# Attention and two MLPs on one core: p stays unnormalised and becomes the stationary operand of P V

## The chip, the cores and the metric

The kernel runs on one core of a Trainium2 chip. The time is the device time of one execution in microseconds (us), and the median of several runs counts. The core has five engines that work side by side: TensorE (PE) for matrix products, VectorE (DVE), ScalarE (ACT), GpSimd (POOL), and SyncE (SP), which here only starts transfers. Each engine takes its own instructions in the order in which they stand in its queue. PE writes its products to PSUM, eight banks of 128 partitions by 512 f32 columns; DVE and ACT read them there. A matrix product loads one operand into PE first (the stationary one, a weight load), and then streams the columns of the other (the moving one) past it.

## The reference

There are 4 batches, 8 heads, 576 positions and 64 columns to a head. Causal attention with a decay goes into two MLPs of 2304 tokens, one after the other:

```python
decay = cum[:, :, :, None] - cum[:, :, None, :]        # cum = cumsum(log(clip(f)))
scores = np.where(causal, -1e9, scale * q @ k.T + decay)
attn = np.exp(scores - scores.max(-1))
attn = attn / (attn.sum(-1) + 1e-09)
x = (attn @ v)                                         # to 2304 x 512
h = x @ w_in                                           # 512 -> 2048
x = (np.maximum(h, 0) + alpha * np.minimum(h, 0)) @ w_out
out = ((x @ w_a) * (x @ w_b)) @ w_o                    # 512 -> 1536 -> 512
```

## The kernel before

The program has three parts: attention together with the first 7 of the 16 column blocks of the first MLP (up to about 362 us; the MLP of the last batch follows until about 412), the other 9 blocks, and the second MLP. The change touches attention alone.

The 32 heads run through slots `u`, one head to a slot. A head has five blocks of queries: 0 to 3 with 128 queries each, and a rest of 64 that is worked on together with the rest of the head's pair (block 4, two heads, 128 rows). For a block, PE makes the scores (`sc`, `scr`), DVE masks them and finds the greatest (line 375, it writes `s` and `nm`), and ACT takes exp of `s` and sums the rows into `sm` (line 376). In the next slot `rinv` makes the reciprocal of the sums, `p_hi` scales `s` by it, and `p_lo` brings P into the form that P V needs: keys on partitions. There are two ways.

- The first ten heads (`NATIVE`) work in f32: `p_hi` scales `s` in place on POOL or ACT, `p_lo` calls `p_whole`, where PE transposes P block by block (`tp`) and ACT or DVE copies it out of PSUM into `PT`. `pv_whole` holds V as the stationary operand (64 columns of V and 64 zeros, so that the two heads of a pair fall on the two halves of the partitions of one bank) and streams P's columns.
- The other 22 heads split P into two f16 parts: `p_hi` writes `s * ri` (times 2^15) as f16 (line 428 on ACT for blocks 2 and 3, line 430 on POOL for 0, 1 and 4), `p_lo` writes what is left of it (line 510, DVE), and a transfer transposes both (line 517). V is split into three bf16 parts by POOL (line 329). `pv` holds two parts of V as the stationary operand and streams P's columns, three matmuls to a block; the result has V's columns on partitions, in two half sums that ACT (line 565) and DVE (line 566) add. For a pair of heads ACT copies the sum to `xh` (line 236), and POOL writes what rounding left to `xl` (line 572).

P V runs two slots behind its head (`LAG`). x then lies with its 512 columns on partitions, and the MLP takes it so: three matmuls in f32r to a product (`mm3`, lines 666 to 668), `leaky` for the sloped step (lines 660 to 663), and `ys` (line 708) out of PSUM.

What runs in which order is set in three layers. Four lists in `_P` (`even0` and `odd0` for the first ten slots, `even` and `odd` for the rest) name the steps of a slot: `s0` to `s3` scores and exp of a block, `R` those of the rest, `ri` and `rr` the reciprocals, `h0` to `h4` and `l0` to `l4` the two halves of P, `p0` and `p1` P V, `T`, `Q`, `V`, `vs` loads and splits, `W` one of 14 weights of the MLP (a transfer, a step of ACT at line 129, three of DVE, then ACT and POOL), `M` the place where MLP steps go in from slot 10 on. `rates` says how much of the MLP goes into a slot. The compiler's scheduler then sets the order of each engine's queue by these places and by its own estimate of when things are ready.

Of the kernel before, what the change touches and what calls it, by code (L numbers as in the profile page):

```python
# [8 lines left out]
F32 = mybir.dt.float32  # L9
# [17 lines left out]
ST = 512  # L27
# [10 lines left out]
    even="ri T h3 h2 h0 s2 vs M h1 Q s0 M l2 s3 M s1 l1 M l0 l3 p0 p1 V po M W".split(),  # L38
    odd="ri h3 h2 h0 R rr vs h1 M Q l2 T l3 s2 M h4 s3 l1 M M s1 l0 s0 p0 p1 V W po l4 M".split(),
# [44 lines left out]
def decay_attention_then_two_mlps(ctx, tc, q, k, v, f, w_in, w_out, alpha, w_a, w_b, w_o, out):  # L84
# [157 lines left out]
    def attention_setup():  # L242
# [19 lines left out]
        for i in range(2):  # L262
# [53 lines left out]
    def load_v(n):  # L316
        b, h = divmod(n, H)
        vs = ap_["vs", n % 3]
        i = 3 if n < NATIVE and n % 2 == 0 else 1
        sp.dma_start(vs[:, 0:4, i], v[b, h, 0:ST].rearrange("(t p) d -> p t d", p=128))  # L320
        sp.dma_start(vs[0:SR, 4, i], v[b, h, ST:])

    def split_v(n):

        if n < NATIVE:
            return
        vs = ap_["vs", n % 3]
        for i in range(1, 3):
            eng(f"v{i}", "pool").tensor_tensor(vs[:, :, i + 1], vs[:, :, i], high(vs[:, :, i]), op=ALU.subtract)
# [20 lines left out]
    def s_view(n, i):  # L350
        if i == 4:
            return ap_["sr"]
        o = {3: 0, 2: 512, 1: 896, 0: 1152}[i]
        return ap_["s", n % 2][:, o:o + 128 * (i + 1)]
# [109 lines left out]

    def pv_whole(u, c):

        g, j = divmod(u, 2)
        vs = ap_["vs", u % 3]
        vz = vs[:, :, 0:2] if j else vs[:, :, 3:5]
        vz = vz.rearrange("p t i d -> p t (i d)")  # L470
        if j == 0:
            ps_x[g, c] = ps["mm"].tile([128, 512], F32, tag="mm", name=f"pvw_{g}_{c}")
        ps_o = ps_x[g, c]
        pt = P32[u, ("lo", "hi")[c]]
        w = 256 + SR * c
        todo_ = []
        for t in range(2 * c + 1):
            b0 = 2 * t + c
            todo_.append((ps_o[:, 0:256].rearrange("p (i n) -> p i n", i=2), t, pt[:, b0:b0 + 2]))
        t = 2 * c + 1  # L480
        todo_.append((ps_o[:, 128:256], t, pt[:, 0 if c else 2]))
        if c == 1:
            qs = slice(SR * j, SR * j + SR)
            for t in range(NQ):
                todo_.append((ps_o[:, 256:w], t, P32[u | 1, "r"][:, t, qs]))
        for m, (o, t, p) in enumerate(todo_):
            first, last = j == 0 and m == 0, j == 1 and m == len(todo_) - 1
            pe.matmul(o, vz[:, t], p, start=first, stop=last, skip_group_check=True)
        if j == 0:
            return  # L490
        b, hp = divmod(g, NP)
        x_tiles(b)
        xh, xl = (x_[:, hp, 256 * c:256 * c + w] for x_ in X[b])
        act.activation(xh, ps_o[:, :w], AF.Copy, scale=1.0 / PSCALE)
        dve.scalar_tensor_tensor(xl, ps_o[:, :w], 1.0 / PSCALE, f32(xh), op0=ALU.mult, op1=ALU.subtract)
# [9 lines left out]
    def p_lo(n, i):  # L505
        if n < NATIVE:
            return p_whole(n, i)
        t, s, ri = p16.pop((n, i))
        g, o = GROUP[i]
        eng(f"l{i}", "dve").scalar_tensor_tensor(t[:, 1::2, :], s, ri, t[:, 0::2, :], op0=ALU.mult, op1=ALU.subtract)  # L510
        whole, done_ = p16[n, g]
        done_.append(i)
        if g == "r" or len(done_) == 2:
            PT[n, g] = ap_["a2"].tile(
                [128, GSIZE[g], 128], F16, tag=f"PT_{g}", name=f"PT_{n}_{g}", bufs=2 if g == "r" else LAG,
            )
            sp.dma_start_transpose(out=PT[n, g], in_=whole.rearrange("p t n -> p (t n)"))
            del p16[n, g]
# [570 lines left out]
```

## Time and profile before

| | us |
|---|---|
| median of 3 runs | 1061.34 (1060.59 to 1064.08) |
| the profiled execution | 1064.5 |
| its span in the profile | 1062.7 |
| PE busy | 1006.4 (95%) |
| weight loads busy | 942.2 (89%) |
| DVE busy | 715.6 (67%) |
| ACT busy | 474.2 (45%) |
| POOL busy | 465.9 (44%) |

Busy times are of the profiled execution, shares are of its span. A busy share is a mean over stages, and a wait that an engine ended is put down to the one that came last. Records of PE overlap: the length of one holds the time until its last result is out, so what one costs in a row of them is the step from one start to the next. An f32 product stands as two records.

### The profile page before, as it was taken

How to read it: one execution, taken by the hardware profiler on the slowest of the kernel's cores; microseconds unless marked ns; L12 is line 12 of the kernel's file. 1: busy time of each engine (PE TensorE's matmuls, PEld its weight loads, DVE VectorE, ACT ScalarE, POOL GpSimd, SP SyncE). 2: the span in 40 equal slices, each digit the busy share in tenths (PEclk: the TensorE clock that was granted, in tenths of full speed). 3: DMA queues.
4: the chain of work that ended last, by engine and by line, in shares of the span. 5: the costliest groups of instructions: out<-in, count | busy, mean ns of one | idle time of the engine just before them, and what ended most of it. 6: DMA issues, size and time to landing. Idle time of an engine off the chain costs nothing.

```text
span 1062.7 us, 17909 instructions
## 1 busy us (share of the span) xinstructions
PE 1006.4 (95%) x6255; PEld 942.2 (89%) x6255; DVE 715.6 (67%) x1463; ACT 474.2 (45%) x1090; POOL 465.9 (44%) x503
## 2 busy tenths in 40 slices
PE   4899899998998999999999998999999999999998
PEld 2777789988898898999999998899989999899997
DVE  5667899679878466444456659755985658965553
ACT  4666788577776554333343443322432113321110
POOL 5344556355455355333456767522543224531111
PEclk9999999999999999999999999999999999999999
DMA  6654588888797676756667996726238383353623
GB/s 137 162 140 152 141 166 169 210 169 170 191 170 155 192 241 209 236 191 191 197 223 263 346 360 237 317 90 239 96 100 317 113 309 121 120 204 142 248 89 109
DMA packets 193582, 202.71 MB, mean 191 GB/s; under 512 B 103956, under 2 KB 160788, under 8 KB 193492
## 3 DMA queue, kind: packets, MB, share of 16 engines
q1 hardware_dynamic: 193492, 201.57, 63.2%
q8 instruction: 49, 0.80, 0.3%
q14 instruction: 41, 0.34, 0.1%
HBM read 133.32 MB, written 50.17 MB: 173 GB/s over the span
## 4 chain that ended last, share of the span: by engine, by line
PE 54%; DVE 7%; DMA 4%; issue 2%; ACT 2%; POOL 2%; SPq 0%; DVEq 0%; ACTq 0%; POOLq 0%
PE p L666 7%; PE p L668 7%; PE p L667 7%; PE o L668 4%; PE o L666 4%; PE o L667 4%; PE ya L666 3%; PE ya L667 3%; PE ya L668 3%; PE hb L668 3%; PE hb L667 3%; PE hb L666 3%; DMA wr_in<-in_moe_w_in 1%; DMA wr_out<-in_moe_w_out 1%; POOL yhl L873 1%
## 5 line engine op out<-in xcount | busy, mean ns | idle before, releaser
L666 PE MATMUL p<-yq,w_h 128*128 128x384 f32 x360 | 121.9, 339 | 2.2 <-DVE lu L1035 1.3
L668 PE MATMUL p<-yq,w_h 128*128 128x384 f32 x360 | 121.3, 337 | 0.0
L667 PE MATMUL p<-yq,w_h 128*128 128x384 f32 x360 | 121.2, 337 | 0.0
L1017 POOL TENSOR_TENSOR gg<-tc,gg 128x384 fp32r<-128x384 f32 x36 | 36.6, 1017 | 113.5 <-ACT gg L1016 96.4
L666 PE MATMUL o<-w_o,gg 128*128 128x512 f32 x216 | 84.7, 393 | 1.7 <-ACT gg L1016 1.7
L376 ACT ACTIVATE s<-s,nm 128x256 f32<-128x256 f32 (+3 forms) x128 | 71.0, 556 | 31.0 <-DVE nm L375 30.5
L667 PE MATMUL o<-w_o,gg 128*128 128x512 f32 x216 | 84.8, 393 | 0.0
L668 PE MATMUL o<-w_o,gg 128*128 128x512 f32 x216 | 83.2, 393 | 0.0
L663 POOL TENSOR_TENSOR gb<-lt,gb 128x384 fp32r<-128x384 f32 x54 | 55.7, 1032 | 60.0 <-ACT gb L662 59.9
L1017 POOL TENSOR_TENSOR gg<-td,gg 128x384 fp32r<-128x384 f32 x36 | 38.0, 1056 | 89.9 <-ACT gg L1016 84.2
L1016 ACT CAST gg<-tc 128x384 fp32r<-128x384 f32 x36 | 18.5, 514 | 124.3 <-DVE tc L1015 123.8
L666 PEld LDWEIGHTS p<-yq,w_h 128*128 128x128 f32 x360 | 67.6, 188 | 7.1 <-DVE lu L1035 1.7
L666 PE MATMUL ya<-gb,w_out 128*128 128x384 f32 x216 | 71.2, 337 | 2.8 <-ACT gb L662 1.6
L667 PE MATMUL ya<-gb,w_out 128*128 128x384 f32 x216 | 72.7, 337 | 0.0
L668 PE MATMUL ya<-gb,w_out 128*128 128x384 f32 x216 | 72.5, 336 | 0.0
L666 PE MATMUL h<-xh,w_in 128*128 128x288 f32 x224 | 66.9, 303 | 5.8 <-ACT ys L708 2.6
L667 PEld LDWEIGHTS p<-yq,w_h 128*128 128x128 f32 x360 | 67.6, 188 | 3.7
L661 DVE SCALAR_TENSOR_TENSOR lt<-lu,nal,hb 128x384 f32<-128x384 f32 x54 | 33.0, 611 | 55.9 <-ACT lu L660 54.2
L663 POOL TENSOR_TENSOR g<-lt,g 128x288 fp32r<-128x288 f32 x56 | 51.0, 916 | 39.0 <-ACT g L662 37.8
L668 PEld LDWEIGHTS p<-yq,w_h 128*128 128x128 f32 x360 | 67.6, 188 | 0.2
L667 PE MATMUL y<-g,w_out 128*128 128x288 f32 x224 | 65.8, 299 | 1.1 <-POOL g L663 1.1
L667 PE MATMUL h<-xl,w_in 128*128 128x288 f32 x224 | 66.1, 296 | 0.0
(202 smaller groups left out, 3238.7 us busy)
## 6 DMA issues: line engine op xcount, KB each, us to landing
yq<-yq_d SPq DMA_DIRECT2D x49, 768.0 KB
yq_d<-yhl SPq DMA_DIRECT2D x42, 384.0 KB
yl<-ya_d SPq DMA_DIRECT2D x48, 192.0 KB
po_d<-os SPq DMA_DIRECT2D x36, 256.0 KB
os<-po_d SPq DMA_DIRECT2D x36, 256.0 KB
wr_in<-in_moe_w_in SPq DMA_DIRECT2D x16, 512.0 KB
wr_out<-in_moe_w_out SPq DMA_DIRECT2D x16, 512.0 KB
RK<-in_k SPq DMA_DIRECT2D x44, 144.0 KB
```

The source lines that it names most:

```text
L376: act.activation(s, s, AF.Exp, bias=nm, scale=-1.0, accum_out=sm)
L661: dve.scalar_tensor_tensor(t, u, nal[:, fi:fi + 1], hp[:, :n], op0=ALU.mult, op1=ALU.add)
L663: pool.tensor_tensor(gl, t, f32(gh), op=ALU.subtract)
L666: pe.matmul(o, lh, rh, start=start, stop=False)
L667: pe.matmul(o, lh, rl, start=False, stop=False)
L668: pe.matmul(o, ll, rh, start=False, stop=stop)
L873: pool.tensor_tensor(yh[:, 1], x, f32(yh[:, 0]), op=ALU.subtract)
L1016: ap_["last"] = act.copy(g[:, 0], o).ins
L1017: pool.tensor_tensor(g[:, 1], o, f32(g[:, 0]), op=ALU.subtract)
```

## The change

P stays as exp left it, and the division comes behind P V. P is now the stationary operand: `pv` loads a block of transposed P (128 keys by 128 queries) and streams 64 columns of V, so x comes out with queries on partitions. All blocks of a head fall into one bank. DVE scales them out of PSUM by the reciprocal, which now has a value to each partition (`xn`), and the rest's 64 rows of each head into one quarter of `xr`. A new step `X`, a slot after a pair's last P V, calls `turn`: PE transposes `xn` (four blocks of 128x128) and multiplies `xr` with `fold`, which puts the two heads' halves side by side; ACT and DVE write `xh` and `xl` out of PSUM. In heads 0 to 9 `p_hi` does nothing. In the others it is one step for blocks 2 and 3 (`hi`, 896 columns, ACT), one for 0 and 1 (`lo`, 384, ACT) and one for the rest (`r`, POOL), and `p_lo` has the same three on DVE. V loses its zeros. The lists in `_P` place the steps anew, and one more slot runs at the end.

```diff
-    even="ri T h3 h2 h0 s2 vs M h1 Q s0 M l2 s3 M s1 l1 M l0 l3 p0 p1 V po M W".split(),
+    even="T h3 h2 h0 h1 s2 vs M Q X s0 M l3 l2 s3 ri M s1 l1 l0 M p0 p1 V M W".split(),
-    eng={'xl': 'pool', 'h2': 'act', 'h3': 'act', 'h0': 'pool', 'h1': 'pool', 'x': 'dve'},
+    eng={'hi': 'act', 'lo': 'act', 'r': 'pool'},
...
+            ap_["xr", i] = a.tile([128, 128], F32, tag=f"xr_{i}", name=f"xr_{i}")
+            zeros(ap_["xr", i])
+        fold = ap_["fold"] = a.tile([128, 64], F32, name="fold")
+        pool.tensor_tensor(fold, ap_["ident"][:, 0:64], ap_["ident"][:, 64:128], op=ALU.add)
...
-            ap_["vs", i] = a.tile([128, NQ, 5, D], F32, tag=f"vs_{i}", name=f"vs_{i}")
-            zeros(ap_["vs", i][:, :, 0::4])
-            zeros(ap_["vs", i][SR:, 4, 1:4])
+            ap_["vs", i] = a.tile([128, 3, NQ, D], F32, tag=f"vs_{i}", name=f"vs_{i}")
+            zeros(ap_["vs", i][SR:, :, 4])
...
     def p_hi(n, i):
...
-                act.activation(s, s, AF.Copy, scale=ri)
...
+        p16.setdefault((n, g, "hi"), []).append(i)
+        if g != "r" and len(p16[n, g, "hi"]) < 2:
+            return
...
-            act.activation(t[:, 0::2, :], s, AF.Copy, scale=ri)
+            act.activation(t[:, 0::2, :], p_view(n, g), AF.Copy, scale=PSCALE)
...
     def p_lo(n, i):
...
-        eng(f"l{i}", "dve").scalar_tensor_tensor(t[:, 1::2, :], s, ri, t[:, 0::2, :], op0=ALU.mult, op1=ALU.subtract)
...
+        dve.scalar_tensor_tensor(
+            t[:, 1::2, :], p_view(n, g), PSCALE, t[:, 0::2, :], op0=ALU.mult, op1=ALU.subtract,
+        )
...
     def pv(u, c):
...
+        def products(o, m, grp, b, t, start, stop):
+            if u < NATIVE:
+                pe.matmul(o, P32[m, grp][:, b], vs[:, 0, t], start=start, stop=stop)
+                return
+            ph, pl = PT[m, grp][:, 2 * b], PT[m, grp][:, 2 * b + 1]
+            parts = [(ph, 0), (ph, 1), (ph, 2), (pl, 0), (pl, 1)]
+            for x, (p, i) in enumerate(parts):
+                pe.matmul(o, p, high(vs[:, i, t]), start=start and x == 0, stop=stop and x == len(parts) - 1)
+
+        for i in (2 * c, 2 * c + 1):
+            for t in range(i + 1):
+                products(ps_o[:, D * i:D * i + D], u, GROUP[i], FIRST[i] + t, t, t == 0, t == i)
+        if c == 0:
+            return
+        for t in range(NQ):
+            products(ps_o[:, 4 * D:5 * D], u | 1, "r", t, t, t == 0, t == NQ - 1)
...
+        dve.tensor_tensor(xs[g][:, :, j], ps_o[:, 0:4 * D].rearrange("p (i d) -> p i d", d=D), ri, op=ALU.mult)
+        a = slice(64 * j, 64 * j + 64)
+        dve.tensor_scalar(
+            ap_["xr", g % 2][a, a], ps_o[a, 4 * D:5 * D], ap_["rir", g % 2][a], 1.0, op0=ALU.mult, op1=ALU.mult,
+        )
...
+    def turn(g):
...
+        for c in range(2):
+            w = 256 + SR * c
+            pt = bank(f"tx_{g}_{c}")[:, :w]
+            for m in range(2):
+                pe.transpose(pt[:, 128 * m:128 * m + 128], xn[:, 2 * c + m].rearrange("p j d -> p (j d)"), ap_["ident"])
+            if c:
+                pe.matmul(pt[:, 256:w], ap_["xr", g % 2], ap_["fold"], start=True, stop=True)
+            xh, xl = (x_[:, hp, 256 * c:256 * c + w] for x_ in X[b])
+            act.copy(xh, pt)
+            dve.tensor_tensor(xl, pt, f32(xh), op=ALU.subtract)
...
-        for u in range(NI + LAG):
+        for u in range(NI + LAG + 1):
...
+                elif op == "X":
+                    if cur(u - 4):
+                        turn((u - 4) // 2)
```

In PE's queue, P V of head 2 stands between the scores of head 4 (`sc`) and the transposes of the rest (`tp_4`). Before (`pvw` is P V's bank, P streams, V is loaded):

```order
L439 MATMUL tp_4_0_467<-ident,sr 128x128 x3
L488 MATMUL pvw_0_483<-PT_2_lo,vs_180 128x256
L488 MATMUL pvw_0_483<-PT_2_lo,vs_180 128x128
L488 MATMUL pvw_1_522<-PT_2_hi,vs_180 128x256 x3
L488 MATMUL pvw_1_522<-PT_2_hi,vs_180 128x128
L439 MATMUL tp_4_3_472<-ident,sr 128x128 x2
L359 MATMUL sc_3_478<-N_103 128x512
L359 MATMUL sc_2_488<-N_103 128x384
L359 MATMUL sc_0_493<-N_103 128x128
```

Now (`pv` is the bank, V streams, P is loaded; `tx` is the turn of heads 0 and 1):

```order
L500 MATMUL pv_478<-vs_185,PT_2_lo 128x64 x3
L362 MATMUL sc_2_482<-N_103 128x384
L500 MATMUL pv_478<-vs_185,PT_2_hi 128x64
L362 MATMUL sc_0_486<-N_103 128x128
L500 MATMUL pv_478<-vs_185,PT_2_hi 128x64 x5
L533 MATMUL tx_0_494<-ident,xn_366 128x128 x2
L500 MATMUL pv_478<-vs_185,PT_2_hi 128x64
L533 MATMUL tx_1_499<-ident,xn_366 128x128 x2
L535 MATMUL tx_1_499<-fold,xr_159 128x64
L500 MATMUL pv_478<-vs_185,PT_3_r 128x64 x4
```

Two matmuls with 256 and 128 columns and four more like them have become ten with 64; the turn of the pair before stands among them, and the transposes of the rest stand ahead of them.

In DVE's queue, these are the steps of head 22 from the row sums on, and the step for head 20's P V. Before (`p_22` is P's low part, `x_10` the sum of half sums):

```order
L398 TENSOR_SCALAR sm_156<-sm_156 128x4
L399 RECIPROCAL ri_157<-sm_156 128x4
L661 SCALAR_TENSOR_TENSOR lt_3066<-lu_3067,nal,h_288_2_2998 128x288
L510 SCALAR_TENSOR_TENSOR p_22_lo<-s_154,ri_157,p_22_lo 128x128
L566 SCALAR_TENSOR_TENSOR x_10_0_3030<-pv_0_3023,x_10_0_3030 64x256
L510 SCALAR_TENSOR_TENSOR p_22_lo<-s_154,ri_157,p_22_lo 128x2x128
L510 SCALAR_TENSOR_TENSOR p_22_hi<-s_154,ri_157,p_22_hi 128x4x128
L510 SCALAR_TENSOR_TENSOR p_22_hi<-s_154,ri_157,p_22_hi 128x3x128
L566 SCALAR_TENSOR_TENSOR x_10_1_3061<-pv_1_3033,x_10_1_3061 64x320
```

Now, for the same heads (`xn` and `xr` are the scaled x of head 20):

```order
L401 TENSOR_SCALAR sm_156<-sm_156 128x4
L481 SCALAR_TENSOR_TENSOR p_22_hi<-s_154,p_22_hi 128x7x128
L481 SCALAR_TENSOR_TENSOR p_22_lo<-s_154,p_22_lo 128x3x128
L517 TENSOR_TENSOR xn_3524<-pv_3448,ri_157 128x4x64
L519 TENSOR_SCALAR xr_159<-pv_3448,rir_158 64x64
L402 RECIPROCAL ri_157<-sm_156 128x4
L623 SCALAR_TENSOR_TENSOR lt_3555<-lu_3556,nal,h_288_2_3441 128x288
```

Four steps for P's low part have become two that read no reciprocal; the reciprocal has moved behind them and behind the scaling of head 20, which reads the older value in the same tile.

## Rows read from the trace of the kernel before

**Rows 1.** Stages: us; PE, PEld, DVE, ACT, POOL busy; PEclk; DMA share; GB/s.
```profile
13.14:53.00 39.86, 34.45 (x171) 26.32 (x172) 26.43 (x90) 24.60 (x63) 14.34 (x24) 0.96 0.67 165
53.00:118.00 65.00, 60.10 (x362) 50.13 (x361) 45.48 (x143) 43.79 (x115) 27.51 (x36) 1.00 0.47 139
118.00:162.00 44.00, 37.27 (x297) 33.85 (x296) 42.65 (x110) 35.75 (x91) 22.41 (x26) 0.92 0.83 167
162.00:362.00 200.00, 186.69 (x1649) 176.74 (x1648) 160.91 (x401) 146.06 (x373) 103.47 (x132) 1.00 0.80 171
362.00:416.00 54.00, 52.11 (x375) 51.27 (x374) 32.05 (x46) 26.66 (x59) 26.68 (x25) 1.00 0.70 233
```

**Rows 2.** What PE waited for, 13.2 to 53: total us, times, longest.
```profile
PE sc L359 <- ACT PT_hi L236: 1.7, 1, 1.7
PE tp L439 <- ACT s L415: 1.3, 2, 0.7
```

**Rows 3.** What PE waited for, 118 to 162 us.
```profile
PE pv L532 <- DMA PT_lo<-p_lo: 2.6, 1, 2.6
PE pv L532 <- DMA PT_hi<-p_hi: 2.5, 2, 1.6
```

**Rows 4.** What PE waited for, 162 to 362 us.
```profile
PE h L666 <- ACT ys L708: 2.6, 3, 1.2
PE pv L532 <- DVE nm L375: 2.1, 3, 1.5
PE h L666 <- DVE lt L661: 1.9, 2, 1.5
PE sc L363 <- DMA TU<-cum_d: 1.3, 1, 1.3
```

**Rows 5.** Timeline of PE, one early head: start, us, instruction, count.
```profile
33.76 0.82 PE L488 MATMUL pvw<-PT_lo,vs 128*128 128x256 f32 x4
35.93 1.23 PE L488 MATMUL pvw<-PT_r,vs 128*128 128x64 f32 x10
36.99 0.93 PE L439 MATMUL tp<-ident,s 128*128 128x128 f32 x7
37.77 1.67 PE L359 MATMUL sc<-N 128*128 128x512 f32 x4
```

**Rows 6.** Timeline of PE, one later head: first, first of 64 columns, next work.
```profile
199.59 0.28 PE L532 MATMUL pv<-PT_lo,vs 128*128 128x256 f16 x1
201.25 0.19 PE L532 MATMUL pv<-PT_r,vs 128*128 128x64 f16 x1
201.68 0.38 PE L666 MATMUL h<-xh,w_in 128*128 128x288 f32 x1
```

**Rows 7.** Weight loads of V: duration min/median/max ns, first and last start.
```profile
L532 PEld LDWEIGHTS <-vs x242: 96/98/147, 124.9 to 359.4; 128*128 128x128 bf16 x121
```

**Rows 8.** Groups by line, 0 to 362 us: busy, mean ns | idle before.
```profile
L510 DVE SCALAR_TENSOR_TENSOR p_hi<-s,ri,p_hi 128x512 f16<-128x512 f32 (+1 forms) x44 | 37.2, 862 | 1.1 <-ACT p_hi L428 1.0
L510 DVE SCALAR_TENSOR_TENSOR p_lo<-s,ri,p_lo 128x128 f16<-128x128 f32 (+1 forms) x44 | 25.8, 591 | 3.4 <-POOL p_lo L430 3.1
L566 DVE SCALAR_TENSOR_TENSOR x<-pv,x 64x256 f32<-64x256 f32 (+1 forms) x44 | 19.9, 453 | 8.3 <-ACT x L565 7.6
L572 POOL TENSOR_TENSOR xl<-x,xh 128x256 fp32r<-128x256 f32 (+1 forms) x22 | 20.2, 922 | 15.7 <-ACT xh L236 15.6
L565 ACT ACTIVATE x<-pv 64x256 f32<-64x256 f32 (+1 forms) x44 | 17.8, 405 | 3.7 <-PE pv L534 2.7
L428 ACT ACTIVATE p_hi<-s,ri 128x512 f16<-128x512 f32 (+1 forms) x44 | 27.1, 660 | 2.5 <-ACT s L376 1.5 <-ACT ys L708 0.6 <-ACT x L565 0.4
```

**Rows 9.** Line 510 by tile: duration min/median/max ns.
```profile
L510 DVE SCALAR_TENSOR_TENSOR p_lo<-s,ri,p_lo x44: 314/520/1409, 122.2 to 351.4; 128x128 f16<-128x128 f32 x22, 128x256 f16<-128x256 f32 x22
L510 DVE SCALAR_TENSOR_TENSOR p_hi<-s,ri,p_hi x44: 583/744/1320, 122.4 to 351.8; 128x512 f16<-128x512 f32 x22, 128x384 f16<-128x384 f32 x22
```

**Rows 10.** Timeline of ACT at the PSUM copy of 40.93 us.
```profile
40.05 0.66 ACT L129 ACTIVATE wx_in<-wr_in 128x512 f32<-128x512 f32 x1 [1.93 <-DMA wr_in<-in_moe_w_in]
```

More of the change, by code (lines that the diff above doesn't have):

```diff
@@ L318, in load_v @@
         vs = ap_["vs", n % 3]
-        i = 3 if n < NATIVE and n % 2 == 0 else 1
-        sp.dma_start(vs[:, 0:4, i], v[b, h, 0:ST].rearrange("(t p) d -> p t d", p=128))
-        sp.dma_start(vs[0:SR, 4, i], v[b, h, ST:])
+        sp.dma_start(vs[:, 0, 0:4], v[b, h, 0:ST].rearrange("(t p) d -> p t d", p=128))
+        sp.dma_start(vs[0:SR, 0, 4], v[b, h, ST:])
     def split_v(n):
@@ L327, in split_v @@
         vs = ap_["vs", n % 3]
-        for i in range(1, 3):
-            eng(f"v{i}", "pool").tensor_tensor(vs[:, :, i + 1], vs[:, :, i], high(vs[:, :, i]), op=ALU.subtract)
+        for i in range(2):
+            pool.tensor_tensor(vs[:, i + 1], vs[:, i], high(vs[:, i]), op=ALU.subtract)
     def bank(nm):
@@ L352, in s_view @@
             return ap_["sr"]
[L353 removed]
+        o = {2: 0, 3: 384, 0: 896, 1: 1024}[i]
         return ap_["s", n % 2][:, o:o + 128 * (i + 1)]
@@ L455, in p_whole @@
         elif i == 2:
-            transposed(n, g, [(2, t) for t in range(3)], slice(1, 6, 2))
+            transposed(n, g, [(2, t) for t in range(3)], slice(0, 3))
         elif i == 3:
-            transposed(n, g, [(3, t) for t in (3, 0, 1, 2)], slice(0, 7, 2))
+            transposed(n, g, [(3, t) for t in range(4)], slice(3, 7))
         else:
@@ L463, in decay_attention_then_two_mlps @@
     ps_x = {}
[L465 to L495, printed above, removed]
     def x_tiles(b):
@@ L507, in p_lo @@
             return p_whole(n, i)
-        t, s, ri = p16.pop((n, i))
-        g, o = GROUP[i]
-        eng(f"l{i}", "dve").scalar_tensor_tensor(t[:, 1::2, :], s, ri, t[:, 0::2, :], op0=ALU.mult, op1=ALU.subtract)
-        whole, done_ = p16[n, g]
+        g = GROUP[i]
+        done_ = p16.setdefault((n, g, "lo"), [])
         done_.append(i)
[L513 to L518, printed above, removed]
+        if g != "r" and len(done_) < 2:
+            return
@@ L520, in pv @@
+        t = p16.pop((n, g))
+        dve.scalar_tensor_tensor(
+            t[:, 1::2, :], p_view(n, g), PSCALE, t[:, 0::2, :], op0=ALU.mult, op1=ALU.subtract,
+        )
+        PT[n, g] = ap_["a2"].tile(
+            [128, 2 * GSIZE[g], 128], F16, tag=f"PT_{g}", name=f"PT_{n}_{g}", bufs=2 if g == "r" else LAG,
+        )
+        sp.dma_start_transpose(out=PT[n, g], in_=t.rearrange("p t n -> p (t n)"))
     def pv(u, c):
-        if u < NATIVE:
-            return pv_whole(u, c)
         g, j = divmod(u, 2)
@@ L525, in pv @@
         vs = ap_["vs", u % 3]
-        ps_o = bank(f"pv_{u}_{c}")
-        v12 = high(vs[:, :, 1:3].rearrange("p t i d -> p t (i d)"))
-        v3 = high(vs[:, :, 3:5].rearrange("p t i d -> p t (i d)"))
-        h0 = 256 * c
-        def passes(o, t, ph, pl, start, stop):
-            pe.matmul(o, v12[:, t], ph, start=start, stop=False)
-            pe.matmul(o, v3[:, t], ph, start=False, stop=False)
-            pe.matmul(o, v12[:, t], pl, start=False, stop=stop)
-        pt = PT[u, ("lo", "hi")[c]]
@@ L567, in pv @@
-        if j == 0:
-            return
-        x_tiles(b)
-        xh, xl = (x_[:, hp, h0:h0 + w] for x_ in X[b])
-        dup(eng("xh", "act"), xh, x32)
-        eng("xl", "pool").tensor_tensor(xl, x32, f32(xh), op=ALU.subtract)
-    xs = {}
-    def pv_out(u):
-        b, h = divmod(u, H)
-        if h == H - 1:
-            bs = slice(b * S, b * S + S)
-            for x_, d in zip(X[b], (xh_d, xl_d)):
-                sp.dma_start(f32(d)[:, :, bs], f32(x_))
-            ready.add(b)
+        if c == 0:
+            pl = "mm" if u < NATIVE else "at"
+            ps_x[u] = ps[pl].tile([128, 512], F32, tag=pl, name=f"pv_{u}")
@@ new lines, in pv @@
+        a = slice(64 * j, 64 * j + 64)
+        dve.tensor_scalar(
+            ap_["xr", g % 2][a, a], ps_o[a, 4 * D:5 * D], ap_["rir", g % 2][a], 1.0, op0=ALU.mult, op1=ALU.mult,
+        )
+    xs = {}
+    def turn(g):
+        b, hp = divmod(g, NP)
+        x_tiles(b)
+        xn = xs.pop(g)
+        for c in range(2):
[8 more added lines that the diff above has]
+            dve.tensor_tensor(xl, pt, f32(xh), op=ALU.subtract)
+        if hp < NP - 1:
+            return
+        bs = slice(b * S, b * S + S)
+        for x_, d in zip(X[b], (xh_d, xl_d)):
+            sp.dma_start(f32(d)[:, :, bs], f32(x_))
+        ready.add(b)
```

91 lines of the change are left out of this document (29 added, 62 removed).

## Prediction

> **What bounds the kernel now.** I began with the table of stages up to the end of attention, where everything lies that the change touches. From 53 us on TensorE (PE) is busy over 90% of the time, except in 118 to 162 us, where VectorE (DVE) is busy 42.65 of 44.00 us and PE only 37.27 [rows 1]. What PE does not work in the first four stages is 5.4, 4.9, 6.7 and 13.3 us, 30.3 us together. To this comes the clock: the mean granted clock is 0.96 and 0.92 of 2.4 GHz in two stages, so parts of them, after PE had waited, ran at the 1.2 GHz level, which took 39.86 x 0.04 = 1.6 and 44.00 x 0.08 = 3.5 us. So at most 35.4 us of this part can be won from PE by shorter waits.
>
> Then the waits of PE. Up to 53 us it waits for a copy of ScalarE (ACT) out of PSUM and for p being scaled (s L415) [rows 2]; in 118 to 162 us for the transposed P [rows 3]; after that for ACT's copy ys, DVE's lt, a transfer of cum_d and a mask step (nm) [rows 4]. Behind attention the work of the last batch fills PE: 52.11 busy of 54.00 us [rows 1]. The MLP steps behind attention keep their number, and so does what comes later; what attention loses or wins goes to the end whole.
>
> **The change part by part.** *TensorE, heads 0 to 9.* A head's P V takes from 33.76 to 36.99, 3.23 us, now. Its five matmuls of 64 columns are ten records (an f32 matmul runs as two) in 36.99 - 35.93 = 1.06 us, 0.106 each [rows 5]. The new head has fifteen of this shape: 15 x 2 x 0.106 = 3.18 us, though it streams 960 columns in place of 1600: at 64 columns the record costs, not the column. Ten heads: -0.5 us.
>
> *TensorE, heads 10 to 31.* Now a head is 33 matmuls in 201.68 - 199.59 = 2.09 us, and the fifteen with 64 columns take 201.68 - 201.25 = 0.43 us, 0.0287 each, each with a load of new weights [rows 6]. The new head is 75 of these: 2.15 us; 22 heads: +1.3 us. What no row shows is a run of 75 in which P (f16) is loaded and V (bf16) streams. From below I bound it by 0.02 us, about a third under the row, from above by 0.098, the load itself if nothing hid it [rows 7]; I take 0.0287, since loads and columns have the same sizes.
>
> A rule speaks against this. The Trainium skill, TensorE: Matmul & The Clock Gate, section Back-to-back issue gap, gives a sustained 81 ns per pair of weight load and matmul at 128 columns, set by both. By it a head would cost 75 x 0.081 = 6.1 us (an estimate from that page). The rows of this trace disagree, with 28.7 ns in a run of fifteen, and the sum goes by them.
>
> *TensorE, turning x.* New, per pair of heads: four transposes and one f32 matmul with 64 columns (two records). Seven transposes take 37.77 - 36.99 = 0.78 us, 0.111 each [rows 5]. So 4 x 0.111 + 2 x 0.106 = 0.656 us, sixteen pairs: +10.5 us. Bounds: nothing, if all of it fell into gaps of PE, and 6 x 0.93 / 7 = 0.80 us a pair, 12.8 in all, with the drain of the last record counted in [rows 5]; I take 0.656, from the very same operation. **PE together: -0.5 + 1.3 + 10.5 = +11.3 us.** Nothing hides this on PE itself; it can only fill the 30.3 us in which PE stands.
>
> *VectorE.* The four steps for the low part of P cost 37.2 + 25.8 = 63.0 us [rows 8], 2.86 a head. They become two with the same columns. The shortest of 128 and of 384 columns, 0.314 and 0.583 us [rows 9], give 1.05 ns a column and 0.18 fixed; so at least two fixed parts go, 0.36 a head, and at most all above 1280 x 1.05 ns + 2 x 0.18 = 1.70, 1.16 a head. I take -0.7: -15 us. For x, 44 steps of 0.45 (19.9 us) [rows 8] and ten like them in heads 0 to 9 go, 24 us; per head come a scaling out of PSUM (0.45, like those), one of 64x64 (below the 0.314 of 128 columns, say 0.2), and half a pair's low parts, 0.45: 1.1 x 32 = 35 us, +11. DVE ends between -15 and +3, say -4; between 118 and 162 us most heads are of the second kind, and each gains 0.7 - 0.2 = 0.5.
>
> Why these steps take so long shows in their spread, 0.314 to 1.409 us [rows 9]. The Trainium skill, SBUF — State Buffer, section SBUF: two separate sides, says that a DVE step with two SBUF inputs and a GpSimd step that reads SBUF exclude each other for a whole instruction. The spread agrees.
>
> *GpSimd and ScalarE.* GpSimd's low part of x (20.2 us) [rows 8] and nearly all its scalings of p go; it bounds nothing. ACT's copies of the half sums go, -17.8 us; its scalings of p, 27.1 us for 896 columns a head in two steps [rows 8], take the other 384 in too, at most 0.66 a head more, +14.5. So it is at most a little lighter.
>
> *The path.* In heads 0 to 9 nothing is scaled between exp and transpose; the wait for s L415 (1.3 us) goes [rows 2], and next come the PSUM copies. In the later heads, P's two parts no longer wait for the reciprocal, but a step of 896 columns must end before its transfer starts, where now two of 512 and 384 follow one another. The new wait is DVE's xn, for the end of P V: behind it in DVE's queue stand mask steps, whose scores PE makes and whose banks it needs; x L566 stands at that place now, and waited 7.6 us for ACT's copy [rows 8], which is gone. The turn waits for xn, but a slot later. GpSimd's early zeros of vs shrink; PE's start waits for transfers, so I count 0.
>
> What PE gets back, by stage: 3.0 of 5.4 + 1.6 (s L415, a part of the copy's 1.7, the clock), 2.5 of 4.9, 6.0 of 6.7 + 3.5 (most of the 2.6 + 2.5 on P's transfers, and of the clock), 5.0 of 13.3 (nm 2.1, the rest what follows x and P). Together 16.5 us, an estimate; none of it is sure, and 35.4 is all there is. **Sum: +11.3 - 16.5 = -5.2 us.** The profiled execution took 1064.5 us (span 1062.7, 1.8 around it), so 1059.3 us; it lies 3.2 above the median of the runs, 1061.3, so their median should come to 1056.1, say 1056.5 us.
>
> **The rivals.** *PE fills and the waits stay* (slower). Place: 162 to 362 us, where PE is busy 186.69 of 200 us. Of its 13.3 us the waits for ys, lt and cum_d make 5.8 [rows 4], and the change touches none of these. Before 53 us, the copy for which PE waits 1.7 us stands in ACT's queue behind a weight that ACT awaits from DRAM (1.93 us) [rows 2, 10], which stays too. If only 4 us come back, it is +7.3, 1068.6 us. It decides from 11.3 us downwards: less regained than this, and the kernel is slower. For it: PE's added work is sure, the gain is not. Against: the DVE-bound 118 to 162 us.
>
> *A draw*: between 8 and 14.5 us come back, one gap filling another; +3.3 to -3.2, about 1061 us. *The chain was the bound all along*: without reciprocal and scaling, and with GpSimd out of DVE's way, 22 us or more come back, -11, 1050 us. For it: DVE at 97% in 118 to 162 us [rows 1]; against: the waits outside of P [rows 4].
>
> *Weight loads not hidden*: each of 75 stands for its 0.098 us [rows 7], 7.35 a head in place of 2.09: 22 x 5.26 = +116, less the 5.2, some 1172 us. Against it: fifteen in 0.43 us [rows 6]. This is the case to which the page's sustained rate leans.
>
> **How the numbers follow.** Forecast (14.5 to 20 us back, 1052.6 to 1058.1): 0.31. Draw: 0.27. PE fills: 0.23. Chain: 0.16. Loads: 0.03. About 0.3%, 3.2 us, is what a measurement can tell from no change. Faster 0.31 + 0.16 = 0.47, same 0.27, slower 0.23 + 0.03 = 0.26. The range goes from 1046, 4 us into the chain's case, to 1069, where the first rival lies; outside I leave the rest of the chain's case, PE regaining nothing (1061.3 + 11.3 = 1072.6), and the loads.
>
> **What will show it.** The 64-column f16 records should follow every 0.029 us; the turn should take 0.66 us a pair. P's low part should come to about 2.1 us a head on DVE. PE's gaps in the stretch of the first later heads (118 to 162 us now) should fall from 6.7 to about 2, with a clock above 0.92, and the last P V should end about 5 us earlier. I am wrong if PE's gaps in the 200 us behind it stay at 13, if PE waits anew for xn or for a bank that the turn holds, or if the pairs of 75 follow at over 0.04 us.

## The result, and the profile after

The changed kernel is slower: 1069.54 us in the median of its runs (1068.32 to 1069.98) beside 1062.57 for the kernel before, a ratio of 1.0065 (95% interval 1.0043 to 1.0087). The forecast was 1056.5. The profiled execution has a span of 1067.5 us, 4.8 more than before; the medians lie 7.0 apart, since the profiled execution before (1064.5 us) was itself 1.9 above its median.

The table of stages of the kernel after answers to [rows 1]: length; PE, PE's loads, DVE, ACT and GpSimd busy, each with its count; the granted clock; the transfers' share of the 16 engines, GB/s. The third stage is 3 us longer here, and the fourth starts 3 us later, as the work does.

```profile
13.14:53.00 39.86, 35.92 (x214) 28.29 (x214) 27.76 (x94) 24.55 (x66) 4.13 (x5) 1.00 0.71 174
53.00:118.00 65.00, 59.47 (x419) 51.97 (x420) 51.51 (x166) 41.22 (x108) 16.32 (x14) 1.00 0.52 145
118.00:165.00 47.00, 41.90 (x461) 40.89 (x460) 34.02 (x82) 29.58 (x75) 18.60 (x20) 0.93 0.69 147
165.00:365.00 200.00, 189.99 (x2456) 185.53 (x2455) 140.35 (x393) 134.06 (x335) 61.50 (x75) 0.97 0.84 169
```

The relief of the other engines came: in 200 us of later heads DVE is busy 140.35 in place of 160.91, GpSimd 61.50 in place of 103.47, ACT 134.06 in place of 146.06. PE is fuller (189.99 in place of 186.69), but its clock, 1.00 there before, is now 0.97. What PE waited for in that stage, in us, times, longest, answers to [rows 4]:

```profile
PE sc L366 <- DMA TU<-cum_d: 5.8, 4, 3.4
PE pv L505 <- DMA PT_lo<-p_lo: 3.1, 2, 2.1
PE y L629 <- POOL g L625: 1.1, 1, 1.1
```

The waits for ys, lt and nm (2.6 + 1.9 + 2.1 us) are gone. In their place stand waits for transfers: cum_d 1.3 before [rows 4], 5.8 now; the transposed P of blocks 0 and 1 (PT_lo) 3.1 now, and before, in the same stage:

```profile
PE pv L532 <- DMA PT_lo<-p_lo: 1.1, 1, 1.1
```

And they come in longer pieces. Two such places, in windows of 2 us (length, PE busy, clock, transfers' share, GB/s; in windows this short the share can pass 1, and nothing is read from that):

```profile
213.00:215.00 2.00, 2.00 (x50) 1.00 1.19 202
215.00:217.00 2.00, 0.35 (x3) 1.00 1.22 227
217.00:219.00 2.00, 0.20 (x1) 0.63 0.83 164
219.00:221.00 2.00, 2.00 (x9) 0.50 0.41 97
221.00:223.00 2.00, 2.00 (x10) 0.50 0.54 127
223.00:225.00 2.00, 2.00 (x12) 0.66 0.97 216
...
300.00:302.00 2.00, 0.17 (x2) 1.00 1.14 335
302.00:304.00 2.00, 1.69 (x40) 0.71 0.65 172
304.00:306.00 2.00, 2.00 (x41) 0.50 0.54 151
```

In the first, PE stands 3.4 us, for cum_d, and then works 5.5 us at the 1.2 GHz level, half of 2.4; in the second it stands 2.1 us, for PT_lo, and 3.4 us of its work run at that level. A third place, at 120 to 124 us, has 7 us at half clock behind a wait for DVE's lt; what PE waited for, 118 to 165 us:

```profile
PE pv L500 <- DVE lt L623: 3.8, 1, 3.8
```

To compare kernels I cut PE's time from 13.14 us to the first matmul of the second MLP (hb) in three: idle is length less busy time, clock is busy time x (1 - granted clock), summed over windows of 1 us, and work is the rest, PE's work at full clock.

| PE from 13.14 us to the first hb | length | idle | clock | idle + clock | work |
|---|---|---|---|---|---|
| before | 392.8 | 30.6 | 4.9 | 35.5 | 357.3 |
| after | 399.6 | 25.0 | 7.9 | 32.9 | 366.7 |

So +9.4 of work, and 2.6 us of waiting given back: +6.8. Behind that point 2.0 us return, and 4.8 stay in the span. How far such figures repeat from profile to profile is read from e5 to e7 below.

### The profile page after: what moved, and what is told of

It reads as the page before. It is cut to its first block, busy times and chain, and to the rows that moved or that the text cites. A ratio compares the mean times of both kernels' runs of the same rounds, so it can differ in the third digit from the quotient of the medians.

```text
span 1067.5 us, 19882 instructions
## 1 busy us (share of the span) xinstructions
PE 1018.4 (95%) x7355; PEld 965.6 (90%) x7355; DVE 694.7 (65%) x1461; ACT 454.7 (43%) x1035; POOL 401.2 (38%) x403
## 4 chain that ended last, share of the span: by engine, by line
PE 66%; DVE 12%; DMA 10%; issue 4%; POOL 3%; ACT 3%; SPq 1%; POOLq 0%; ACTq 0%; DVEq 0%
PE p L628 7%; PE p L630 7%; PE p L629 7%; PE o L630 4%; PE o L628 4%; PE o L629 4%; DMA wr_out<-in_moe_w_out 4%; PE ya L628 3%; PE pv L505 3%; PE ya L629 3%; PE ya L630 3%; PE hb L630 3%; PE hb L629 3%; PE hb L628 3%; DMA wr_in<-in_moe_w_in 2%
## 5 line engine op out<-in xcount | busy, mean ns | idle before, releaser
L379 ACT ACTIVATE s<-s,nm 128x512 f32<-128x512 f32 (+3 forms) x128 | 71.4, 558 | 32.6 <-DVE nm L378 32.1
L332 POOL TENSOR_TENSOR vs<-vs 128x320 f32<-128x320 f32 x44 | 32.8, 745 | 118.7 <-DMA vs<-in_v 86.5
L625 POOL TENSOR_TENSOR g<-lt,g 128x288 fp32r<-128x288 f32 x56 | 54.7, 982 | 55.6 <-ACT g L624 55.6
L629 PE MATMUL y<-g,w_out 128*128 128x288 f32 x224 | 67.2, 303 | 1.5 <-POOL g L625 1.5
L628 PE MATMUL y<-g,w_out 128*128 128x288 f32 x224 | 66.7, 306 | 1.0 <-ACT w_out L137 1.0
```

What stands on the lines that cost most here:

```text
L332: pool.tensor_tensor(vs[:, i + 1], vs[:, i], high(vs[:, i]), op=ALU.subtract)
L379: act.activation(s, s, AF.Exp, bias=nm, scale=-1.0, accum_out=sm)
L625: pool.tensor_tensor(gl, t, f32(gh), op=ALU.subtract)
L628: pe.matmul(o, lh, rh, start=start, stop=False)
L629: pe.matmul(o, lh, rl, start=False, stop=False)
```

## Experiments

Each kernel was timed beside the kernel before; ratios are to it, with their 95% intervals. Idle + clock and work are those of the table above, from one profile each.

| kernel | median us | ratio | idle + clock | work |
|---|---|---|---|---|
| e1 after, x stored by pair | 1071.6 | 1.0081 (1.0059 to 1.0103) | 34.1 | 369.1 |
| e2 before, x stored by pair | 1066.5 | 1.0039 (1.0024 to 1.0053) | 40.1 | 356.1 |
| e3 after, no turn | 1063.4 | 1.0009 (0.9991 to 1.0027) | 32.1 | 359.4 |
| e4 after, four low parts | 1068.7 | 1.0049 (1.0030 to 1.0068) | 32.7 | 368.3 |
| e5 after, v split late | 1069.8 | 1.0062 (1.0039 to 1.0084) | 31.8 | 367.6 |
| e6 e5 and q, k stacked late | 1072.6 | 1.0079 (1.0050 to 1.0108) | 35.7 | 366.9 |
| e7 before, v split late | 1062.3 | 0.9992 (0.9972 to 1.0012) | 33.4 | 357.9 |
| e8 after, q loaded once | 1063.1 | 0.9998 (0.9983 to 1.0014) | 22.8 | 368.6 |
| e9 before, q loaded once | 1064.6 | 1.0017 (1.0001 to 1.0033) | 38.6 | 354.3 |
| e10 after, q and k once | 1055.9 | 0.9932 (0.9912 to 0.9952) | 19.0 | 367.2 |
| e12 before, q and k once | 1067.6 | 1.0048 (1.0031 to 1.0066) | 41.3 | 356.4 |
| e13 e10 and other banks | 1052.6 | 0.9905 (0.9887 to 0.9924) | 15.4 | 367.3 |
| e14 e8 with dummy transfers | 1065.4 | 1.0024 (1.0007 to 1.0041) | 27.7 | 367.9 |

**e1 and e2: x stored by pair.** The first suspect was seen in SP's queue, the timeline of DMA issues (start, us), of the kernel after:

```profile
289.54 0.58 SPq L543 DMA_DIRECT2D xh_d<-xh  x1
290.23 4.50 SPq L487 DMA_TRANSPOSE PT_hi<-p_hi  x1
294.82 1.17 SPq L543 DMA_DIRECT2D xl_d<-xl  x1
296.04 3.44 SPq L487 DMA_TRANSPOSE PT_lo<-p_lo  x1
299.60 0.57 SPq L323 DMA_DIRECT2D vs<-in_v  x1
300.28 0.52 SPq L324 DMA_DIRECT2D vs<-in_v  x1
300.84 0.60 SPq L309 DMA_DIRECT2D RK<-in_k  x1
```

Two transposes of P behind x's stores take 4.50 and 3.44 us to issue, and v and k of the next heads follow only at 299.60 and 300.84; from 300.2 us PE stands, until PT_lo is there at 302.3. Theory A: this is where the gain was lost.

```
-        if hp < NP - 1:
-            return
         bs = slice(b * S, b * S + S)
         for x_, d in zip(X[b], (xh_d, xl_d)):
-            sp.dma_start(f32(d)[:, :, bs], f32(x_))
+            sp.dma_start(f32(d)[:, hp, bs], f32(x_)[:, hp])
...
```

> The kernel after, but each pair of heads stores its own 288 KB of xh and xl right after its turn, in place of 1152 KB each after the last pair of a batch. Theory A (what the change won was lost again at the ends of the batches, where two transposes of P stand behind x's stores in SP's queue and took 4.50 and 3.44 us to issue at 290 and 296 us, so v and k came late): in 209 to 226 and 300 to 312 us PE stood 4.45 + 3.04 us and lost about 3.4 + 1.7 us to the clock, 12.6 in all; half to all of it goes, 1057 to 1063 us, and the transposes issue in under 2 us. Theory B (PE's added work alone, 12 us more busy, makes the kernel slower, and the stalls come from the bytes, however they are cut): within 3 us of the kernel after, 1067 to 1071 us.

> The kernel before with the same edit: x stored by pair. Theory A: its transposes behind the stores took 2.80, 2.58 and 5.21 us as well (201 to 206 and 286 us), but its PE lost no clock there; it gains less than the kernel after, 0 to 5 us, 1056 to 1061 us. Theory B: no change, 1059 to 1064 us.

Theory A found no support. Neither kernel gained: e2 is some 4 us slower, with 24 more issues in SP's queue, outside what either theory expected of it, and e1's 1.7 us more than the kernel after are within the noise. PE still stalls at 214 and 308 us, and newly at 260 (1.8 us busy of 5). But the edit did only a part of what A asked for. At 290 us, in e1:

```profile
291.65 0.53 SPq L541 DMA_DIRECT2D xh_d<-xh  x1
292.28 0.38 SPq L541 DMA_DIRECT2D xl_d<-xl  x1
292.71 3.67 SPq L487 DMA_TRANSPOSE PT_hi<-p_hi  x1
296.44 1.33 SPq L487 DMA_TRANSPOSE PT_lo<-p_lo  x1
297.87 0.53 SPq L323 DMA_DIRECT2D vs<-in_v  x1
```

One of the two transposes still takes over 2 us; v follows 6.2 us behind the start of the stores, 10.1 in the kernel after. And ahead of the stall at 215 us the transposes near x's stores had taken only 1.59 and 2.11 us in the kernel after.

**e3: no turn.** The four transposes and the matmul of each pair are left out, and ACT and DVE read SBUF:

```
-            pt = bank(f"tx_{g}_{c}")[:, :w]
...
-                pe.transpose(pt[:, 128 * m:128 * m + 128], xn[:, 2 * c + m].rearrange("p j d -> p (j d)"), ap_["ident"])
...
-            act.copy(xh, pt)
+                act.copy(xh[:, o:o + n], y)
...
```

> The kernel after without the turn on TensorE: ACT and DVE read xn and xr as they lie, so x is not transposed (that part of the computation is left out; the same number of elements is copied). By the sum of the prediction the turn is 16 x 0.656 = 10.5 us of PE. If PE is full (theories A and B alike): 9 to 12 us less, 1057 to 1061 us. Rival (PE's gaps hide the turn, and the time is lost in the stalls alone): less than 4 us less, above 1065 us.

The work fell by 7.3 us, the time by 6.0 (the difference of the ratios, 0.0056, times 1062.6; its interval is some 3 us to either side), and idle + clock stayed, 32.1 beside 32.9. So most of the turn was not hidden; but its price is below the 9 us expected. ACT and DVE make three copies a pair here in place of two, so e3 is no clean removal.

**e4: four low parts again on DVE.** Each block of queries makes its own low part; the transfers still wait for the whole group.

```
+        t = p16[n, g]
+        lo, hi = FIRST[i], FIRST[i] + (NQ if i == 4 else i + 1)
+        dve.scalar_tensor_tensor(
+            t[:, 2 * lo + 1:2 * hi:2, :], p_view(n, g)[:, lo:hi], PSCALE, t[:, 2 * lo:2 * hi:2, :], ...
+        )
         if g != "r" and len(done_) < 2:
             return
-        t = p16.pop((n, g))
-        dve.scalar_tensor_tensor(
-            t[:, 1::2, :], p_view(n, g), PSCALE, t[:, 0::2, :], ...
...
```

> The kernel after with P's low part in four steps a head again in place of two (each transfer still waits for the whole of its group). Gives VectorE back two fixed parts a head, some 0.4 us, and the shorter steps; 22 heads, 8 to 15 us of DVE. If VectorE's load no longer sets the time anywhere (theories A and B): within 3 us of the kernel after, 1066 to 1072 us. Rival (the chain through VectorE still ends the waits): 5 us or more slower, over 1074 us.

DVE's steps for the low parts (busy, mean ns | idle before) in the kernel after and in e4:

```profile
L481 DVE SCALAR_TENSOR_TENSOR p_hi<-s,p_hi 128x896 f16<-128x896 f32 x22 | 25.0, 1135 | 7.7 <-ACT p_hi L428 7.7
L481 DVE SCALAR_TENSOR_TENSOR p_lo<-s,p_lo 128x384 f16<-128x384 f32 x22 | 13.3, 605 | 0.1
```
```profile
L480 DVE SCALAR_TENSOR_TENSOR p_hi<-s,p_hi 128x512 f16<-128x512 f32 (+1 forms) x44 | 30.4, 728 | 8.0 <-ACT p_hi L428 7.9
L480 DVE SCALAR_TENSOR_TENSOR p_lo<-s,p_lo 128x256 f16<-128x256 f32 (+1 forms) x44 | 15.7, 394 | 1.9 <-ACT p_lo L428 1.8
```

DVE has 7.8 us more to do, and the time stays. So these 7.8 us of DVE's relief decide nothing in the changed kernel.

**e5, e6, e7: the split of v late.** GpSimd waited 86.5 us in 118 to 362 us for v at the head of its queue, 36.1 before, with the MLP's g behind. In the lists of a slot:

```
-even="T h3 h2 h0 h1 s2 vs M Q X s0 M l3 l2 s3 ri M s1 l1 l0 M p0 p1 V M W"
+even="T h3 h2 h0 h1 s2 M Q X s0 M l3 l2 s3 ri M s1 l1 l0 M p0 p1 vs V M W"
```

The odd list and those of the kernel before have the same move; e6 also puts T behind the first M of the even list. Theory C: GpSimd's early stand at v makes DVE and PE wait.

> The kernel after with the split of v (vs) issued at the end of a slot, behind P V, in place of early in it; v is then used two slots later, as now. Theory C (GpSimd, relieved of P and x, reaches vs L332 early and stands there for v's transfer: 86.5 us in 118 to 362, before 36.1; the MLP's g and p_r behind it in its queue make VectorE's low part and lt late, which hold PE's banks): the waits for v at the head of GpSimd's queue go to under 20 us, PE's idle and clock loss of 118 to 362 us (22.9 us) fall by a quarter to a half, and the time falls by 4 to 11 us, to 1058 to 1065. Theory B (PE's work alone; whichever engine waits, another wait takes its place): within 3 us of the kernel after, 1066 to 1072 us.

> As e5, and in even slots the stacking of q and k (T) behind the first mask step of the slot and the first piece of the MLP, so that ACT does not stand at its queue's head for PE's scr or sc of the slot before (12.7 us in 118 to 362). Theory C: 0 to 4 us less than e5. Theory B: as the kernel after, 1066 to 1072 us. Rival: the stacked scores now come too late for the next slot, and PE waits for cum_d or TU more often: 3 us or more slower than e5.

> The kernel before with the split of v at the end of a slot. There GpSimd waits for v 36.1 us in 118 to 362. Theory C: as GpSimd still has P and x to do, less of that wait reaches PE; 0 to 5 us faster, 1057 to 1062 us. Theory B: no change, 1059 to 1065.

None of the three tests theory C. In e5 all five engines have, in the trace, the same operations on the same tiles in the same order as in the kernel after, and in e7 as in the kernel before; in e6 one store of y (`ya_d`) has changed places with a transfer of cum_d in SP's queue, and nothing else has moved. The list of a slot is not the order of a queue.

So they are repeats, and tell how far figures repeat. The ratios of e5 and e6 lie within the noise of the kernel after, that of e7 at 1. GpSimd's wait for v is 113.6 us in e5, 86.5 in the kernel after, at the same time. Work repeats within 1 us (366.7 to 367.6 after, 357.3 and 357.9 before), but idle + clock is 32.9, 31.8 and 35.7 after, 35.5 and 33.4 before: a difference under some 4 us in that column, read from one profile each, shows nothing.

**e8 and e9: q loaded once.** In the stage of the later heads SP does little but issue: 187 issues take 165.0 of the 197 us from 165 to 362 in the kernel after (84%), 186 take 164.2 before. The cum_d for which PE stands from 215.4 us on, in SP's queue:

```profile
213.91 1.59 SPq L487 DMA_TRANSPOSE PT_hi<-p_hi  x1
215.60 0.93 SPq L346 DMA_DIRECT2D TU<-cum_d  x1
```

From 195.5 us up to here the queue had no pause of over 0.5 us; PE goes on at 218.80. Theory D: SP's queue is the second bound behind PE. Each head loads q and k twice, into partitions 0 to 63 and 64 to 127. The second q, 33 transfers in all, can go:

```
-        for tq, tk in homes:
+        for i, (tq, tk) in enumerate(homes):
             sp.dma_start(tk, k[b, h])
+            if i:
+                break
...
-        act.copy(t1, rq)
+        act.copy(t1[0:64], rq[0:64])
-        dve.tensor_tensor(t1[64:128], rq[64:128], f32(t1)[64:128], op=ALU.subtract)
+        dve.tensor_tensor(t1[64:128], rq[0:64], f32(t1)[0:64], op=ALU.subtract)
```

> The kernel after with q of the later heads loaded once: its second copy in partitions 64 to 127 goes (one transfer a head, two in odd heads, 33 of SP's 229 issues in 118 to 365 us, some 0.6 us each, 20 us), and VectorE takes the low part of q from the first copy. All values stay the same, and PE's, ACT's and DVE's counts too. Theory D (SP's queue, which issues 170 of 197 us in the later heads of both kernels, is the second bound behind PE: q and k of the next head, v and the transposes come late whatever the other engines do, so the shorter chain gave nothing back): idle plus clock loss of PE up to the first hb falls from 32.9 to 20 to 27 us, the time by 5 to 12 us, to 1057 to 1065. Theory B (another wait takes its place): within 3 us of the kernel after, 1067 to 1072 us.

> The kernel before with the same edit (q loaded once). Theory D: its queue is as full, 168 of 197 us, so it gains about as much as the kernel after, 4 to 12 us, 1050 to 1058 us. Theory B: within 3 us of before, 1059 to 1065 us. If only the kernel after gains, SP's queue is what the change ran into.

On the kernel after theory D's forecast came: the edit takes off 7.1 us (0.0067 of 1062.6), and idle + clock fall from 32.9 to 22.8, more than the repeats differ; in 165 to 362 us alone they fall from 14.4 to 6.3. On the kernel before it failed. There D expected 4 to 12 us as well, since the queue is as full, and the edit takes off nothing: e9 is 1.8 us slower, by an interval that just leaves out 1. So a queue that issues 84% of the time is not a bound by that alone; it is the changed kernel that ran into its transfers.

**e10 and e12: k loaded once too.** GpSimd copies the rounded k to the other partitions.

```
-        for tq, tk in homes:
+        for i, (tq, tk) in enumerate(homes):
+            if i:
+                break
...
-        act.copy(u1, rk)
+        act.copy(u1[0:64], rk[0:64])
+        pool.tensor_scalar(u1[64:128], f32(u1)[0:64], 1.0, 0.0, op0=ALU.mult, op1=ALU.add)
...
```

> As e8, and k's second copy goes as well: ACT rounds the first into 64 partitions and GpSimd copies that to the other 64, so 22 more issues (13 us of SP) go, and GpSimd has 22 more steps of some 0.8 us. Theory D: 0 to 6 us less than e8. Rival (the copy through GpSimd is late, since it stands behind the split of v and g's low parts): slower than e8 by 2 us or more. Theory B: as the kernel after.

> The kernel before with q and k of the later heads loaded once, as in e10. If SP's queue is what only the changed kernel ran into: no gain, as in e9 (GpSimd, with P and x to do, takes k's copy late), 1060 to 1067 us, so that the change is worth some 7 us or more of gain once SP has room. Rival (fewer transfers of k help any kernel, and e10's lead over e8 has nothing to do with the change): 1053 to 1058 us, as fast as e10.

e10 gains more than expected: 7.0 us below e8 by the ratios, and faster than the kernel before. What its PE waited for in 165 to 362 us:

```profile
PE y L632 <- POOL g L628: 1.5, 2, 1.1
PE tx L536 <- DVE xn L520: 1.1, 3, 0.5
PE sc L369 <- DMA TU<-cum_d: 0.7, 2, 0.4
```

The 5.8 us for cum_d are 0.7, and idle + clock of this stage are 3.8. The same edit makes the kernel before slower by 0.5%. The stage of the later heads, first of e10, then of e12:

```profile
165.00:362.00 197.00, 193.18 (x2507) 188.10 (x2506) 144.79 (x395) 135.51 (x341) 78.27 (x92) 1.00 0.75 164
```
```profile
165.00:362.00 197.00, 185.60 (x1626) 175.98 (x1626) 154.23 (x398) 144.18 (x369) 107.07 (x143) 0.99 0.70 149
```

With the transfers relieved, PE is busy 193.18 of 197 us with the new P V, and 185.60 with the old. Why the old one loses was not followed further; from 13 to 410 us its PE waits 7.7 us for the transposed P of blocks 2 and 3 (PT_hi) in e12 and 11.6 in e9, 2.5 in the kernel before.

**e14: issues or bytes?** e8 with the second transfer of q issued, but 16 columns of it, which nothing reads:

```
+            if i:
+                for m in range(1 + j):
+                    sp.dma_start(tq[:, 64 * m:64 * m + 16], q[b, h, :, 64 * m:64 * m + 16])
+                break
```

> e8 with the second transfer of q issued all the same, but with 16 columns (4 KB) in place of 576 or 512 and 64, which nothing reads: the issues of the kernel after, the bytes of e8. If it is the issues in SP's queue that the kernel after waits for: most of e8's gain goes, 1066 to 1070 us. If it is the bytes (the transfers' share of the engines was 0.84 in 165 to 365 us): as e8, 1061 to 1065 us.

The time lies between the two, 2.8 us above e8 by the ratios (some 1.7 us to either side for each), but it says nothing on the question. Nothing reads what the small transfers bring, and the scheduler issued all 33 of them ahead of the later heads (duration in ns, min/median/max; first and last start in us):

```profile
L312 SPq DMA_DIRECT2D RQ<-in_q x33: 465/547/1035, 29.3 to 89.0; - x33
```

In 165 to 362 us SP's queue has 169 issues in e14, as in e8, and idle + clock are 7.4 us there, beside 6.3 in e8 and 14.4 in the kernel after. What e14 loses against e8 lies before 165 us (19.7 beside 14.8). So in the later heads e14 is e8 once more, and whether the changed kernel waits for the issues or for the bytes stays open.

**e13: other banks for P V of heads 8 and 9.**

```
-            pl = "mm" if u < NATIVE else "at"
+            pl = "mm" if u < 8 else "at"
```

> e10, with P V of heads 8 and 9 in the banks of the scores in place of the three that the MLP's h uses. In e10 PE stands 3.6 us at 116 to 119 for DVE's lt, whose h holds the bank that P V of head 9 wants, and runs 9 us at the half clock after it (4.7 us lost). If this wait is one of banks: 3 to 8 us less than e10, 1048 to 1053 us. Rival (the next wait at that place, w_out or lt itself for h, comes to the same): within 2 us of e10.

In e10, 113 to 130 us, PE waited:

```profile
PE pv L503 <- DVE lt L626: 3.6, 1, 3.6
PE h L631 <- DVE lt L626: 0.7, 1, 0.7
```

and in e13:

```profile
PE tx L536 <- DVE xn L520: 1.9, 1, 1.9
PE y L631 <- ACT w_out L137: 0.7, 1, 0.7
```

The wait for the bank is gone, and one of 1.9 us for xn stands near its place. By the ratios 2.9 us of the time went too, between what the two sides expected; the intervals are some 2 us to either side for each, so this gain is hardly clear of the noise. e13 is the fastest kernel of the study, 0.95% below the kernel before.

## Why the prediction was wrong, step by step

*PE, heads 0 to 9: right.* The timeline of the kernel after, one early head:

```profile
43.22 1.23 PE L500 MATMUL pv<-vs,PT_hi 128*128 128x64 f32 x10
44.29 0.39 PE L533 MATMUL tx<-ident,xn 128*128 128x128 f32 x2
```

Ten records in 44.29 - 43.22 = 1.07 us, 0.107 each, where 0.106 was taken.

*PE, heads 10 to 31: right.* The timeline of the kernel after, a turn and then one later head:

```profile
197.18 0.60 PE L533 MATMUL tx<-ident,xn 128*128 128x128 f32 x4
197.62 0.33 PE L535 MATMUL tx<-fold,xr 128*128 128x64 f32 x2
197.76 0.31 PE L365 MATMUL sc<-U,T 128*128 128x128 f32 x1
...
201.43 1.21 PE L505 MATMUL pv<-vs,PT_hi 128*128 128x64 bf16 x35
202.48 0.91 PE L505 MATMUL pv<-vs,PT_r 128*128 128x64 bf16 x25
```

35 matmuls start within 202.48 - 201.43 = 1.05 us, 0.030 each; 0.0287 was taken from [rows 6]. The rival of loads that aren't hidden is out: P's loads stand in the trace at 98 ns each (busy, mean ns | idle before), and one starts every 30 ns, so they overlap.

```profile
L505 PEld LDWEIGHTS <-PT_hi 128*128 128x128 f16 x770 | 25.3, 98 | 0.1
```

The Trainium skill, TensorE: Matmul & The Clock Gate, section Weight-path perf modes — Fast Weight Load (FWL) and DoubleRow, says that a load of 128 weights of a type other than f32 is split into four chunks that go in parallel. Whether that is at work here, no run tells.

*PE, the turn: a little high.* 197.76 - 197.18 = 0.58 us a pair, not 0.656; e3 prices all 16 at 6.0 us of time and 7.3 of work, not 10.5. PE's work rose by 9.4 us in all, forecast 11.3.

*DVE, GpSimd, ACT: more relief than forecast.* The low parts fell from 63.0 to 25.0 + 13.3 = 38.3 us, by 24.7 and not by 15. DVE as a whole is busy 694.7 us in place of 715.6, where 4 us less were forecast. e4 shows that 7.8 us of this were worth nothing in time.

*What PE gets back: this step failed.* 16.5 us were forecast, 2.6 came in this pair of profiles, and some 1 us with the repeats e5, e6 and e7 (33.5 in the mean of three profiles after, 34.5 in that of two before). Over the same stretches of time, idle + clock in the first pair:

| stage, us | before | after | given back | forecast |
|---|---|---|---|---|
| 13 to 53 | 5.4 + 1.7 | 3.9 + 0.0 | 3.2 | 3.0 |
| 53 to 118 | 4.9 + 0.0 | 5.5 + 0.0 | -0.6 | 2.5 |
| 118 to 165 | 6.7 + 3.2 | 5.1 + 3.4 | 1.4 | 6.0 |
| 165 to 362 | 13.3 + 0.0 | 10.0 + 4.4 | -1.1 | 5.0 |

The last stage alone is short by 6.1 us. There the prediction took each wait by the engine it named, let it go with the step that the engine lost, and left out what would come last then. The waits on engines did go. But q, k, v, cum_d and P's transposes come through one queue that was issuing 83% of the time (164.2 of 197 us), and the change takes no transfer out of it. With the engines earlier, the waits for its transfers took their place, and in longer pieces, so that 4.4 us of clock went with them; in the two profiles before, that stage lost 0.0 and 1.7.

e8 and e10 show it from the other side: taking transfers out gives the changed kernel back 7.1 and 14.1 us, and the kernel before nothing. With q loaded once, this stage does give back 7.0 of its 13.3 us (6.3 are left), where 5.0 were forecast. What the runs leave open is what it is about the transfers: their issuing, their bytes, or their order in the queue, for no run separates the first two, and none puts cum_d ahead of the transposes. That they came last because the engines had become faster is read from the waits.

In 118 to 165 us the waits for P's transfers [rows 3] went as forecast, and another came in their place: the stall at 120 us, 3.8 us for a PSUM bank that the MLP's h holds until lt. P V of heads 8 and 9 takes its bank from the three of the MLP in both kernels. e13 shows for e10 that the wait is one for the bank; on the kernel after itself it was not tried. Why nothing came back in 53 to 118 us was not followed.

*The rivals.* "PE fills and the waits stay" gave 1068.6 us, and 1069.5 came: right in the sum, right that the added work is sure and the gain is not. But it named the waits for ys and lt as those that stay, and these went; it was the third, cum_d, that grew. That its time came so near is in part luck. "The chain was the bound all along" has the result against it, and for the changed kernel e4: 7.8 us more on DVE changed nothing.

*The signs.* Gaps at the first later heads fell to 5.1 and not to 2, the clock there was 0.93 as before (over 118 to 165 us), the last P V came 3.1 us later (362.6 against 359.5), not 5 earlier. P's low part came to 38.3 / 22 = 1.74 us a head, below the 2.1. PE's gaps behind did not stay at 13, they fell to 10.0, but the clock took 4.4; for xn PE waited only 0.9 us.

## What to carry to other kernels

Before counting a wait as won, look at what else comes in at that place, transfers above all: here the queue that issues them was as full after the change as before, and the waits moved to it once the engines were relieved. How full it is does not decide by itself: the kernel before had the same queue and gained nothing from fewer transfers. Work added to an engine that is busy over 90% is paid for the most part (e3: 7.3 us of work, 6.0 of time), while the return of idle time has to be shown wait by wait. A change that loses for such a reason can win once the other bound is moved: e13 is the changed kernel, 1.6% faster. And read in the queues of the trace whether an edit did what it was made for: e5, e6 and e7 had moved next to nothing, and e14 had put its transfers where they tell nothing.

## What was not expected of the hardware

The issue of a plain transfer takes SP's queue 0.64 us in the mean, that of a transpose 1.65 (142 and 45 of them in 165 to 362 us of the kernel after); right behind a store of 1152 KB a transpose took 4.50 us, behind one of 288 KB in e1 3.67. Idle time in long pieces can cost PE twice: behind waits of 3.4 and 2.1 us it worked 5.5 and 3.4 us at half clock, and the 13.3 us of gaps of the later heads before, none over 1.6 us, left the clock at 1.00. But the length of the gap alone does not tell: in e5, with the same queues as the kernel after, one of 2.95 us at 216 us left the clock at 1.00, and one of 1.95 us at 301 us had 3.4 us at half clock behind it. And P as the stationary operand, with a new load for every 64 columns, runs at 0.030 us a matmul over 35 in a row.
